# Attention's token stores on GpSimd's own queue, four units later, into sixteen arrays

## The chip, the cores and the metric

One core of one Trainium2 chip runs the whole program. The metric is the device time of one execution in microseconds (us), the median of several runs.

## The reference, cut to what matters

Attention with a decay bias runs first: 4 batches, 8 heads, 576 positions, head size 64. Its result, as 2304 tokens of width 512, goes through a first expert layer (2048 wide, squared ReLU) and a second one (three input matrices of width 768, of which the maximum is taken).

```python
cum = np.cumsum(np.maximum(s, 0.0), axis=-1)
bias = -(cum[:, :, :, None] - cum[:, :, None, :])
scores = np.where(causal, -1e9, scale * q @ k.T + np.minimum(bias, 0.0))
attn = exp(scores - max) / (sum + 1e-9)
x = (attn @ v).transpose(0, 2, 1, 3).reshape(2304, 512)
h = np.maximum(x @ moe_w_in, 0.0);            x = h * h @ moe_w_out
h = max(x @ w1, x @ w2, x @ w3);              out = h @ w_out
```

## The kernel before, in words

**Attention.** The 32 heads are taken as 16 pairs. A pair has nine units (`NU = 9`), each a block of 64 query rows of both heads (the last unit is the 64 rows of the tail), so there are 144 units. A unit passes through the stages scores (`u_s`), maximum (`u_max`), exponential (`u_exp`), transposition (`u_t`) and copy (`u_et`). Units are gathered in two windows for each pair: window 0 ends at unit 3 and window 1 at unit 8. A window passes through the stages `rc` (reciprocals of the sums), `pv` (the product with the values, L768, and a small transposition, L771), `out0`/`out1` (`w_out_`: VectorE copies the product to a buffer `ax`, L779, and the reciprocals to `rec`, L781), `keep` (SyncE writes the reciprocals to DRAM, L698 and L700), `rows` (SyncE reads them back spread over 128 partitions into a buffer `px`, L707), `px` (GpSimd multiplies `ax` by `px`, L786) and `xst` (the result is stored to the DRAM array `x_at`, L791).

**The order is written out by hand.** A list gives each stage its distance in units: at step n of the loop over units, the stage is issued for the window that ended at unit n + distance.

```python
ORDER = [("max", 1), ("rc", -4), ("out0", -6), ("out1", -7), ("exp", -1), ("et", -3), ("t", -2), ("s", 2), ("pv", -5), ("rows", -15),
         ("pump", 0), ("keep", -8), ("px", -21), ("xst", -23)]
```

Every engine takes its instructions strictly in the order of the program. SyncE (SP) does no arithmetic: in attention its queue holds nearly all transfers, one behind the other. For each pair these are the loads of `xk` (L600) and `xq` (L604), the four decay rows `ck` and `cq` (L611), the values `xv` in two parts (L618, L619), three `keep` writes, four `rows` reads and two `xst` stores. The loads of pair p are issued two pairs ahead, at the steps `LOADS = (1, 1, 2, 15)` counted from unit 0 of pair p - 2; `xv` is the one at 15, so it is issued 3 units before pair p begins, and `pv` of its window 0 comes at unit 3 with a distance of 5, thus 11 units behind that issue.

**Weights.** Beside attention, a planner (`Slots`, called by `pump` on six of nine units from unit 9 on) brings in weights of the first layer: two loads of 256 KB for each weight tile into `st` (L392), some word arithmetic on VectorE (L397 to L408), additions on GpSimd (L415, L433) and a cast on ScalarE (L429). In attention these loads go on SP's queue; from the expert phase on they go on GpSimd's, and the additions go to VectorE for jobs begun then.

**From attention to the experts.** The tokens 0 to 511 are read from `x_at` into `fx` (L817) and split (ScalarE L796, VectorE L799) while attention still runs; the first 24 matmuls of the first layer (L804) are laid between attention's last units. The first layer then visits the token chunks (512, 512, 512, 384, 384) in the order 0 to 4 and back 3 to 0. Each next chunk is read by `xload` (L890), 512 or 384 columns for each of the four feature blocks kk; the reads for the second visit are issued by ScalarE, all others by SP. Matmuls: L804 is the first product, ScalarE and VectorE (L963 to L966) make the squared activations `hh`, L987 is the second product.

`ax` has six buffers and `px` two; the pools of attention and of the experts lie in the same memory, one after the other. `x_at` is one DRAM array of [4, 128, 2304].

Of the kernel before, what the change touches and what calls it, by code (L numbers as in the profile page):

```python
# [8 lines left out]
F32 = mybir.dt.float32  # L9
# [41 lines left out]
PACE = 1.5  # L51
PACE_ATT = 5
ORDER = [("max", 1), ("rc", -4), ("out0", -6), ("out1", -7), ("exp", -1), ("et", -3), ("t", -2), ("s", 2), ("pv", -5), ("rows", -15),
         ("pump", 0), ("keep", -8), ("px", -21), ("xst", -23)]

# [189 lines left out]
def kernel(  # L247
# [15 lines left out]
    nc = tc.nc  # L263
    P = 128
    D = v_tail.shape[2]
    S = qT.shape[2]
    H = 8
    BH = s.shape[0]
    B = BH // H
    NT, DM = out.shape  # L270
    KD = DM // P
# [14 lines left out]

    perm = ctx.enter_context(tc.tile_pool(name="perm", bufs=1))
    dram = ctx.enter_context(tc.tile_pool(name="dram", bufs=1, space=bass.MemoryType.DRAM))
    x_at = dram.tile([KD, P, NT], F32, name="x_at")
    x_mid = dram.tile([KD, P, NT], F32, name="x_mid")  # L290
    part = dram.tile([KD, P, NT], F32, name="part")
    r_dram = [[dram.tile([2, (W0, W1)[w]], F32, name=f"r{w}{i}") for i in range(2)] for w in range(2)]
# [61 lines left out]
    def unit(n, i):  # L354
        _, q, j = items[n]
        return 7 * (3 * q + j) + i
# [141 lines left out]
    queue = [nc.sync]  # L498
# [14 lines left out]
    keep = {i: dram.tile([P, 1024], F32, name="keep_" + "_".join(map(str, i))) for i in second + late}  # L513
# [7 lines left out]
    phA = ExitStack()  # L521
# [1 line left out]
    at1 = phA.enter_context(tc.tile_pool(name="at1", bufs=1))  # L523
    small = phA.enter_context(tc.tile_pool(name="small", bufs=6))
    et_p = phA.enter_context(tc.tile_pool(name="et", bufs=2))
    px_p = phA.enter_context(tc.tile_pool(name="px", bufs=2))
    ax_p = phA.enter_context(tc.tile_pool(name="ax", bufs=6))
    fx_p = phA.enter_context(tc.tile_pool(name="fx", bufs=4))
    ring_s, ring_t = Ring(pairs[2:4]), Ring(pairs[0:2])

# [242 lines left out]
    ax_t = {}  # L773
# [14 lines left out]
    def w_xst(p, w):  # L788
        lo, hi = ((0, W0), (W0, S))[w]
        b, h = divmod(2 * p, H)  # L790
        nc.sync.dma_start(out=x_at[h // 2, :, b * S + lo:b * S + hi], in_=ax_t.pop((p, w))[:, 0:hi - lo])  # L791

    three = ((0, 0), (0, 1), (1, 0))

    def high(x, hi):
        nc.scalar.copy(out=hi, in_=x)  # L796

    def low_of(x, hi, lo):
        nc.vector.tensor_tensor(out=lo, in0=x, in1=f32(hi), op=ALU.subtract)  # L799
# [11 lines left out]
    fx = {}  # L811

    def first_split(kk, step):
        t0, n = chunks1[0]
        if step == 0:
            fx[kk] = fx_p.tile([P, 512], F32, tag="fx", name="fx")[:, 0:n]
            nc.sync.dma_start(out=fx[kk], in_=x_at[kk, :, t0:t0 + n])  # L817
        elif step == 1:
            first_x[kk] = tuple(slots_a[-1 - kk][:, i, :] for i in range(2))
            high(fx[kk], first_x[kk][0][:, 0:n])  # L820
        else:
            low_of(fx[kk], first_x[kk][0][:, 0:n], first_x[kk][1][:, 0:n])
# [5 lines left out]
    def attention():  # L828
# [3 lines left out]
        N = len(units)  # L832
        fns = dict(s=u_s, t=u_t, max=u_max, et=u_et, exp=u_exp)
        wfn = dict(rc=w_rc, pv=w_pv, out0=w_out_, out1=w_out_, keep=w_keep, rows=w_rows, px=w_px, xst=w_xst)
        span = max(abs(d) for _, d in ORDER)
        pre = first_products()
        coming = {}
        for n in range(-span, N + span + 1):
            if 0 <= n < N:
                p = n // NU  # L840
                for back in range(3):
                    if p + 2 - back < NP and p >= back:
                        to = p + 2 - back
                        if n == (to - 2) * NU + LOADS[0]:
                            coming[to] = loads(to)
                        for at, f in zip(LOADS, coming.get(to, ())):
                            if n == (to - 2) * NU + at:
                                f()
            for op, d in ORDER:
                if op == "pump":  # L850
                    if PUMP_FROM <= n < N + PUMP_END and n % NU in PUMP_U and (slots.free or slots.open):
                        slots.pump(1)
                elif op in wfn:
                    if n + d in wins and op not in ("out1", "out0")[wins[n + d][1]]:
                        wfn[op](*wins[n + d])
                elif 0 <= n + d < N:
                    fns[op](n + d)
            if n == N - PRE_AT:
                phQ.close()
                banks.extend(psum(ctx, "first", 2, [P, 512]))  # L860
            for kk in range(KD):
                for step, off in enumerate((-24, 0, 1)):
                    if n == N - PRE_X[kk] + off:
                        first_split(kk, step)
            if n >= N - PRE_AT:
                for _ in range(PRE_N):
                    next(pre, None)
# [3 lines left out]
    def experts():  # L871
# [15 lines left out]

        def xload(at, t0, n, kk):
            x = xr[at, kk] = xr_p.tile([P, 2 * T2], F32, tag="xr", name="xr")[:, 0:n]
            (nc.scalar if at == 1 else nc.sync).dma_start(out=x, in_=x_at[kk, :, t0:t0 + n])  # L890

        def xsplit(at, n, kk):
            x = xr.pop((at, kk))
# [29 lines left out]
        with ExitStack() as ph1:  # L923
# [11 lines left out]
            for kind, v, m, f in main1:  # L935
                ci, fs = visits[v]
                t0, n = chunks1[ci]
                end = m == len(fs) - 1
                nxt = chunks1[visits[v + 1][0]] if v + 1 < nv else None
                if kind == "h":  # L940
                    w = slots.get(("in", f))
# [8 lines left out]
                    if nxt:  # L950
                        for kk in range(KD):
                            if to_end == 7 - kk:
                                xload(v + 1, *nxt, kk)
                    elif to_end == 7:
                        for i in range(4):
                            raw_load(0, i)
# [12 lines left out]
                    if to_end in (5, 3):  # L969
                        kk = (5 - to_end) // 2  # L970
# [9 lines left out]
                else:  # L980
                    w = slots.get(("out", f))
# [30 lines left out]
        with ExitStack() as ph2:  # L1012
# [5 lines left out]
            at = {}  # L1018
# [91 lines left out]
            for item in main2:  # L1110
                if item[0] == "p":
                    _, m, i = item
# [3 lines left out]
                    b = where[i]  # L1116
                    if (m, b) not in at:
                        at[m, b] = rings[b].take()
                    w = slots.get(("p", unit(m, i) // 2))
                    at_w = unit(m, i) % 2 * 256  # L1120
                    x = ops[g, i]
# [16 lines left out]
                else:  # L1138
                    _, g, t, f, begin, end = item
# [69 lines left out]
```

## Time and profile before

| what | value |
|---|---|
| median of 3 runs | 859.21 us (856.16 to 860.18) |
| profiled execution, own time | 855.43 us |
| its span (first to last instruction) | 853.5 us, so 1.93 us lie around the span |
| granted TensorE clock, mean | 0.996 of full speed |
| attention with its last windows | about 0 to 191 us of the span |
| first layer's stream of matmuls | about 171 to 574 us |
| second layer | about 574 to 853 us |

The profile is one execution. Times in its rows are counted from the span's start. PE is TensorE, PEld its weight loads, DVE VectorE, ACT ScalarE, POOL GpSimd, SP SyncE; a trailing q means the engine's queue of instructions. L and a number is a line of the kernel.

### The profile page before, as it was taken

How to read it: one execution, taken by the hardware profiler on the slowest of the kernel's cores; microseconds unless marked ns; L12 is line 12 of the kernel's file. 1: busy time of each engine (PE TensorE's matmuls, PEld its weight loads, DVE VectorE, ACT ScalarE, POOL GpSimd, SP SyncE). 2: the span in 40 equal slices, each digit the busy share in tenths (PEclk: the TensorE clock that was granted, in tenths of full speed). 3: DMA queues.
4: the chain of work that ended last, by engine and by line, in shares of the span. 5: the costliest groups of instructions: out<-in, count | busy, mean ns of one | idle time of the engine just before them, and what ended most of it. 6: DMA issues, size and time to landing. Idle time of an engine off the chain costs nothing.

```text
span 853.5 us, 14429 instructions
## 1 busy us (share of the span) xinstructions
PE 829.5 (97%) x5284; PEld 702.8 (82%) x5284; DVE 525.6 (62%) x1103; ACT 408.4 (48%) x833; POOL 157.2 (18%) x241
## 2 busy tenths in 40 slices
PE   5999998898999999999999999999999999999998
PEld 3555554577888899999998888889998899989996
DVE  6778786837885566676687786753564235623442
ACT  5888887854544444445554454442233222421222
POOL 3042323325122333213222313100000000000000
PEclk9999999999999999999999999999999999999999
DMA  5555556544344553697658677729930573026602
GB/s 161 175 173 174 165 176 201 164 129 155 127 168 143 200 205 129 242 374 277 226 181 302 229 274 244 251 84 390 406 139 25 198 264 131 13 74 201 242 1 74
DMA packets 72246, 159.76 MB, mean 187 GB/s; under 512 B 11376, under 2 KB 31408, under 8 KB 72176
## 3 DMA queue, kind: packets, MB, share of 16 engines
q1 hardware_dynamic: 56340, 106.40, 36.2%
q0 software_dynamic: 15248, 51.39, 17.3%
q10 hardware_dynamic: 588, 1.06, 0.5%
q8 instruction: 41, 0.67, 0.3%
q14 instruction: 29, 0.24, 0.1%
HBM read 113.53 MB, written 45.27 MB: 186 GB/s over the span
## 4 chain that ended last, share of the span: by engine, by line
PE 88%; DMA 4%; DVE 3%; ACT 2%; SPq 1%; issue 1%; POOL 1%; ACTq 0%; POOLq 0%; DVEq 0%
PE banks L987 22%; PE banks L1124 13%; PE banks L804 11%; PE first L804 10%; PE banks L1096 9%; PE first L1124 8%; PE pairs L768 5%; PE pairs L723 3%; PE pair L644 2%; PE pairs L644 2%; DMA px<-r 1%; DMA st<-in_w_out_dram 1%; DMA xq<-in_qT_dram 1%; SPq L707 1%; PE pair L651 1%; PE pairs L651 1%
## 5 line engine op out<-in xcount | busy, mean ns | idle before, releaser
L987 PE MATMUL banks<-hh,sl 128*128 128x512 f32 (+1 forms) x960 | 211.6, 369 | 2.5 <-DVE hh L966 2.5
L987 PEld LDWEIGHTS banks<-hh,sl 128*128 128x128 f32 x960 | 176.1, 189 | 25.8 <-DVE hh L966 2.9
L1124 PE MATMUL banks<-xs,sl 128*128 128x384 f32 x702 | 131.2, 335 | 0.0
L1124 PEld LDWEIGHTS banks<-xs,sl 128*128 128x128 f32 x702 | 122.8, 188 | 0.9 <-DMA sl<-keep_p 0.2
L966 DVE TENSOR_TENSOR hh<-r,hh 128x512 fp32r<-128x512 f32 (+1 forms) x80 | 52.4, 656 | 99.6 <-ACT hh L965 99.4
L804 PE MATMUL first<-xs,sl 128*128 128x512 f32 (+1 forms) x432 | 93.6, 365 | 0.0
L804 PE MATMUL banks<-xs,sl 128*128 128x512 f32 (+1 forms) x432 | 93.6, 365 | 0.0
L681 ACT ACTIVATE e<-e,nm 128x128 f32<-128x128 f32 (+2 forms) x144 | 83.6, 585 | 12.3 <-DVE nm L667 12.1
L804 PEld LDWEIGHTS first<-xs,sl 128*128 128x128 f32 x432 | 78.6, 188 | 9.4
L804 PEld LDWEIGHTS banks<-xs,sl 128*128 128x128 f32 x432 | 78.6, 188 | 9.4
L1124 PE MATMUL first<-xs,sl 128*128 128x384 f32 x432 | 84.6, 335 | 0.0
L1096 PE MATMUL banks<-sl,hh 128*128 128x512 f32 (+1 forms) x342 | 78.4, 382 | 1.9 <-DVE hh L799 1.5
L1124 PEld LDWEIGHTS first<-xs,sl 128*128 128x128 f32 x432 | 75.8, 188 | 0.7 <-issue 0.3
L1096 PEld LDWEIGHTS banks<-sl,hh 128*128 128x128 f32 x342 | 61.4, 188 | 15.9 <-DVE hh L799 3.4
L963 ACT ACTIVATE r<-banks 128x512 f32<-128x512 f32 (+1 forms) x40 | 22.2, 556 | 93.9 <-PE banks L804 86.1
L963 ACT ACTIVATE r<-first 128x512 f32<-128x512 f32 (+1 forms) x40 | 22.2, 556 | 89.9 <-PE first L804 88.9
L768 PEld LDWEIGHTS pairs<-et,xv 128*64 128x64 f32 (+1 forms) x448 | 28.2, 136 | 34.8 <-ACT e L681 8.9
L768 PE MATMUL pairs<-et,xv 128*64 128x320 f32 (+4 forms) x448 | 53.2, 370 | 3.6 <-DVE nm L667 3.6
L1025 ACT COPY s<-first 128x384 f32<-128x384 f32 x36 | 17.2, 479 | 79.3 <-PE first L1124 79.2
L786 POOL TENSOR_TENSOR ax<-ax,px 128x256 f32<-128x256 f32 (+1 forms) x32 | 26.9, 840 | 120.6 <-DMA px<-r 93.8
L1025 ACT COPY s<-banks 128x384 f32<-128x384 f32 x45 | 21.6, 479 | 57.0 <-PE banks L1124 56.5
L964 ACT ACTIVATE r<-r 128x512 f32<-128x512 f32 (+1 forms) x80 | 47.2, 590 | 2.6
(108 smaller groups left out, 1154.6 us busy)
## 6 DMA issues: line engine op xcount, KB each, us to landing
sl<-keep_p SPq DMA_DIRECT2D x68, 512.0 KB
st<-in_w_dram POOLq DMA_DIRECT2D x36, 256.0 KB, 5.7
st<-in_w_out_dram POOLq DMA_DIRECT2D x35, 256.0 KB, 3.9
sl<-keep_out SPq DMA_DIRECT2D x14, 512.0 KB
keep_p<-hi POOLq DMA_DIRECT2D x9, 768.0 KB, 5.2
keep_p<-sums POOLq DMA_DIRECT2D x9, 768.0 KB, 6.1
st<-in_w_in_dram POOLq DMA_DIRECT2D x22, 256.0 KB, 4.2
xk<-in_kT_dram SPq DMA_DIRECT2D x16, 288.0 KB
```

Source lines behind the costliest of these rows:

```text
L644: nc.tensor.matmul(b[:, j, 0:w], lhsT=d["xq"][rows(j), w - P:w], rhs=d["xk"][rows(j), 0:w], start=True, stop=False)
L681: nc.scalar.activation(out=e_u[u][:, 0:w], in_=e_u[u][:, 0:w], func=ACTF.Exp, scale=-1.0, bias=st.pop(n), accum_out=sums[p, win][:, col:co ...
L768: nc.tensor.matmul(pv[rows(j), f:(W0, W1)[w]], lhsT=xv[0:kr, j, k, :], rhs=rhs, start=(k == 0), stop=(k == last))
L786: nc.gpsimd.tensor_tensor(out=x[:, 0:n], in0=x[:, 0:n], in1=rs_t.pop((p, w))[:, 0:n], op=ALU.mult)
L804: nc.tensor.matmul(hps[:, 0:n], lhsT=w[:, wp, kk * P:(kk + 1) * P], rhs=x[kk][xp][:, 0:n], start=(kk == 0 and c == 0), stop=(kk == KD - 1 ...
L963: nc.scalar.activation(out=r[:, 0:n], in_=hps[:, 0:n], func=ACTF.Relu)
L964: nc.scalar.activation(out=r[:, 0:n], in_=r[:, 0:n], func=ACTF.Square)
L966: nc.vector.tensor_tensor(out=hh[:, 1, 0:n], in0=r[:, 0:n], in1=f32(hh[:, 0, 0:n]), op=ALU.subtract)
L987: nc.tensor.matmul(xacc[d][:, 0:n], lhsT=w[:, wp, d * P:(d + 1) * P], rhs=hh[:, xp, 0:n], start=(m == 0 and c == 0), stop=(end and c == 2))
L1025: nc.scalar.copy(out=x, in_=bank[:, 0:T2])
L1096: nc.tensor.matmul(b, lhsT=hh[g, t][:, hp_, q, h, :], rhs=w[:, wp, lo:hi], start=(begin and n == h == c == 0), stop=(end and n == len(f) - ...
L1124: nc.tensor.matmul(at[m, b][:, 0:T2], lhsT=w[:, wp, at_w + kk * P:at_w + (kk + 1) * P], rhs=x[:, kk, xp, :], start=(i in (0, 1, 3) and kk ...
```

## The change

`px` and `xst` are both issued 25 units behind their window (they were at 21 and 23). The store goes on GpSimd's own queue instead of SP's, right behind the multiplication. `ax` gets eight buffers in place of six, `px` three in place of two. `x_at` becomes sixteen arrays [128, 576], by feature block (kk) and batch; so a read of tokens is cut at each multiple of 576 by a new function `tokens`, and chunks 1, 2 and 3 take two transfers for each block where they took one. `xload` uses SP's queue for all visits.

```diff
-         ("pump", 0), ("keep", -8), ("px", -21), ("xst", -23)]
+         ("pump", 0), ("keep", -8), ("px", -25), ("xst", -25)]
...
-    x_at = dram.tile([KD, P, NT], F32, name="x_at")
+    x_at = [[dram.tile([P, S], F32, name=f"x_at{k}{b}") for b in range(B)] for k in range(KD)]
...
-    px_p = phA.enter_context(tc.tile_pool(name="px", bufs=2))
-    ax_p = phA.enter_context(tc.tile_pool(name="ax", bufs=6))
+    px_p = phA.enter_context(tc.tile_pool(name="px", bufs=3))
+    ax_p = phA.enter_context(tc.tile_pool(name="ax", bufs=8))
...
-        nc.sync.dma_start(out=x_at[h // 2, :, b * S + lo:b * S + hi], in_=ax_t.pop((p, w))[:, 0:hi - lo])
+        nc.gpsimd.dma_start(out=x_at[h // 2][b][:, lo:hi], in_=ax_t.pop((p, w))[:, 0:hi - lo])
+
+    def tokens(queue, x, kk, t0, n):
+        at = t0
+        while at < t0 + n:
+            b, lo = divmod(at, S)
+            m = min(S - lo, t0 + n - at)
+            queue.dma_start(out=x[:, at - t0:at - t0 + m], in_=x_at[kk][b][:, lo:lo + m])
+            at += m
...
-            nc.sync.dma_start(out=fx[kk], in_=x_at[kk, :, t0:t0 + n])
+            tokens(nc.sync, fx[kk], kk, t0, n)
...
-            (nc.scalar if at == 1 else nc.sync).dma_start(out=x, in_=x_at[kk, :, t0:t0 + n])
+            tokens(nc.sync, x, kk, t0, n)
```

## Rows read from the trace of the kernel before

**Rows 1.** Part 1 of the page: busy us, share of span, instructions

```profile
PE 829.5 (97%) x5284; PEld 702.8 (82%) x5284; DVE 525.6 (62%) x1103; ACT 408.4 (48%) x833; POOL 157.2 (18%) x241
```

**Rows 2.** Windows in the expert phase: length, busy us by engine, PEclk, DMA

```profile
205.00:315.00 110.00, 110.00 (x490) 91.77 (x490) 79.28 (x138) 54.92 (x96) 28.45 (x54) 1.00 0.47 161
```

**Rows 3.** Windows from pair to pair (PE, PEld, DVE, ACT, POOL busy, PEclk, DMA)

```profile
119.22:128.81 9.59, 9.44 (x119) 5.60 (x119) 7.81 (x30) 8.62 (x26) 3.31 (x4) 1.00 0.52 148
128.81:143.44 14.63, 11.05 (x120) 6.82 (x119) 8.99 (x26) 10.03 (x27) 4.32 (x5) 0.88 0.64 201
143.44:155.44 12.00, 10.14 (x122) 5.93 (x122) 8.53 (x35) 9.68 (x26) 2.83 (x3) 1.00 0.67 192
155.44:165.56 10.12, 9.77 (x121) 5.74 (x122) 8.68 (x32) 8.19 (x23) 4.13 (x5) 1.00 0.51 156
...
sum 155.80, PE 149.18 PEld 89.45 DVE 115.71 ACT 130.71 POOL 46.12; mean PE 9.95 PEld 5.96 DVE 7.71 ACT 8.71 POOL 3.08
```

**Rows 4.** Timeline of PE, 120 to 160 us (start, us, ...)

```profile
133.62 0.22 PE L646 MATMUL pair<-ck,cq 64*128 64x128 bf16 x2
137.42 1.39 PE L768 MATMUL pairs<-et,xv 128*64 128x256 f32 x8 [3.58 <-DVE nm L667]
...
154.10 1.13 PE L644 MATMUL pair<-xk,xq 64*128 64x512 f32 x4 [1.48 <-DVE nm L667]
```

**Rows 5.** Timeline of ACT, 126 to 142 us

```profile
134.31 0.78 ACT L745 COPY et<-pairs 128x768 f32<-128x768 f32 x1
```

**Rows 6.** Timeline of SP's queue, attention

```profile
28.61 0.53 SPq L600 DMA_DIRECT2D xk<-in_kT_dram  x1
...
130.45 0.34 SPq L791 DMA_DIRECT2D x_at<-ax  x1
131.10 1.12 SPq L707 DMA_DIRECT2D px<-r  x2
132.32 0.53 SPq L618 DMA_DIRECT2D xv<-in_v_main_dram  x1
...
148.38 0.58 SPq L392 DMA_DIRECT2D st<-in_w_out_dram  x1
149.06 0.38 SPq L600 DMA_DIRECT2D xk<-in_kT_dram  x1
```

**Rows 7.** Timeline of DVE, 126 to 166 us

```profile
133.39 0.49 DVE L779 COPY ax<-pairs 128x320 f32<-128x320 f32 x1 [1.82 <-DMA x_at<-ax]
...
152.79 0.57 DVE L397 TENSOR_SCALAR wa<-st 128x512 uint32<-128x512 uint32 x1 [1.83 <-DMA st<-in_w_out_dram]
```

**Rows 8.** The line L791: duration in ns min/median/max, first and last start

```profile
L791 SPq DMA_DIRECT2D x_at<-ax x32: 325/341/525, 37.1 to 191.2; - x32
```

**Rows 9.** Waits of SP's queue: total us, times, longest

```profile
SPq L791 <- POOL ax L786: 5.9, 7, 2.9
```

**Rows 10.** The line L392 from 190 us on: GpSimd's own DMA issues

```profile
L392 POOL DMA_DIRECT2D st<-in_w_out_dram x35: 536/541/739, 192.4 to 542.4; - x35
```

**Rows 11.** The tile ax: GpSimd's multiplications

```profile
L786 POOL TENSOR_TENSOR ax<-ax,px x32: 726/859/1522, 30.7 to 190.3; 128x256 f32<-128x256 f32 x16, 128x320 f32<-128x320 f32 x16
```

**Rows 12.** Window in the expert phase where VectorE is full

```profile
215.00:220.00 5.00, 5.00 (x23) 4.14 (x23) 4.90 (x10) 2.38 (x4) 1.06 (x2) 1.00 0.31 105
```

**Rows 13.** Timeline of POOL, end of attention

```profile
190.32 0.88 POOL L786 TENSOR_TENSOR ax<-ax,px 128x320 f32<-128x320 f32 x1 [2.45 <-DMA px<-r]
191.15 1.29 POOL L433 TENSOR_TENSOR sl<-wa,sl 128x512 fp32r<-128x512 f32 x1
192.38 0.74 POOL L392 DMA_DIRECT2D st<-in_w_out_dram  x1
```

**Rows 14.** Timeline of DVE, 170 to 215 us

```profile
197.03 0.43 DVE L397 TENSOR_SCALAR wa<-st 128x512 uint32<-128x512 uint32 x1 [6.94 <-DMA st<-in_w_out_dram]
```

**Rows 15.** Timeline of PE, 165 to 215 us

```profile
202.88 4.18 PE L987 MATMUL banks<-hh,sl 128*128 128x512 f32 x11 [2.52 <-DVE hh L966]
```

**Rows 16.** Timeline of ACT, 170 to 215 us

```profile
185.31 0.60 ACT L963 ACTIVATE r<-banks 128x512 f32<-128x512 f32 x1 [4.27 <-DMA x_at<-ax]
```

## The prediction

> **What bounds the kernel now.** I read the page first. TensorE is busy for 829.5 of 853.5 us [rows 1], so only 24 us of the span can be won without changing its work. The windows of the expert phase show where they are not: over 110 us there PE is busy for all 110 [rows 2]. Whatever this change moves in the expert phase is therefore hidden as long as no wait grows to reach PE. The idle time must lie at the start (nothing here touches it), in attention, or between the two phases.
>
> Next I cut attention into windows from one pair's long `pv` product to the next [rows 3]. A pair takes about 9.6 us, PE full nearly throughout; the first row is the last such pair (9.59). The next three take 14.63, 12.00 and 10.12 us for the same work. Against 9.6 each they lose 5.03 + 2.40 + 0.52 = 7.95 us. In the worst one the granted clock falls to 0.88, between its two levels of 2.4 and 1.2 GHz, after PE had stood still: part of the 5.03 is slower work behind the wait.
>
> Then I asked what PE waited for there. The timeline of PE has two gaps: 3.58 us before an L768 at 137.42 and 1.48 us before an L644 at 154.10 [rows 4], both put down to VectorE's maximum. For the first that name can't be the cause: L768 reads `et` and `xv`, and no maximum. ScalarE's copy to `et` ended at 134.31 + 0.78 = 135.09 [rows 5]. What is left is `xv`, and SP's queue issued its load only at 132.32 [rows 6], 5.1 us before the product began. By the code the issue lies 11 units ahead of that product, at 9.6 / 9 = 1.07 us a unit 11.7 us; the product was due at 133.84, behind the last matmuls before the gap [rows 4], so the load was due at 122.1 and SP was 10.2 us late.
>
> Why is it late? Its `xk` loads, one for each pair, stand at 28.61 and, eleven pairs on, at 149.06 [rows 6]: (149.06 - 28.61) / 11 = 10.95 us a pair, where TensorE needs 9.6. SP falls behind by 1.35 us with each pair, and where the queue is read closely its issues stand nearly end to end [rows 6]. It eats up the distance by which loads were issued early, and from pair 12 on TensorE pays.
>
> The second gap has the same root by another way: VectorE stood for 1.83 us before L397 for a weight load [rows 7], issued on SP at 148.38 [rows 6], and the maximum that PE needed is behind L397. A third sign: VectorE stood for 1.82 us before L779, for a store of `x_at` that had to free one of the six `ax` buffers [rows 7].
>
> **The change part by part.**
>
> *Stores leave SP's queue.* 32 of them, two for each pair, of median 0.34 us [rows 8], and with them SP's waits for the multiplication, 5.9 us in all, or 0.37 for each of 16 pairs [rows 9]. SP's pace becomes 10.95 - 0.68 = 10.27 us by the issues alone and 9.90 with the waits. The lateness at pair 12, 10.2 us, shrinks in the ratio of the excess over 9.6: to 10.2 x 0.67 / 1.35 = 5.1 us, or 2.3. The load of `xv` then has 11.7 - 5.1 = 6.6 us or more, and needed 5.1. The weight load came 1.83 us too late for L397 and would come at least 5.1 earlier. Both gaps go, and with them the 0.52: -7.95 us.
>
> *Two more `ax` buffers and one more `px`.* A window holds `ax` from 6 or 7 to 25 units behind it, and the eighth next window comes 36 units later, so L779 finds a free buffer: the 1.82 us on VectorE go (they are inside the 7.95). `rows` of the third next window comes 13 or 14 units later, at 28 units from this one against its `px` at 25. That leaves SP 3 units, as before (24 against 21).
>
> *`px` four units later.* GpSimd's wait for `rows` moves into time in which SP is late anyway; nothing queues behind it in those units but additions for the weights. Costed at nothing; without that cover ScalarE's cast L429 and all behind it would wait.
>
> *The stores on GpSimd.* Such an issue takes 0.541 us there in the median, 0.739 at the most [rows 10]. GpSimd works 46.12 us over 15 pairs, 3.08 a pair [rows 3]; two stores make it 4.2 of 9.6. So it has room. One place has none: the last multiplication at 190.32 is followed by an addition and by the first weight load of the expert phase at 192.38 [rows 13]. VectorE stands 6.94 us for that load [rows 14], and behind it TensorE stands 2.52 us for `hh` [rows 15]. The last store comes between them, and every us there reaches PE: one issue of 0.54 and about 0.1 for the multiplication's end. The bounds are nothing (if the last `rows` arrives sooner) and 1.52, the longest thing that GpSimd did with that tile [rows 11]; I take 0.65, as the issue has rows of its own.
>
> Does GpSimd issue at 0.54 us while VectorE is busy? In the window at 215 VectorE works 4.90 of 5 us and GpSimd's 1.06 us there are two issues [rows 12], with the same word arithmetic as in attention. The Trainium skill (SBUF — State Buffer, SBUF: two separate sides) says that a GpSimd-issued DMA can be kept from writing its descriptors by a VectorE instruction in a two-port mode, and gives about 3100 ns in place of 620; its summary says to issue such a DMA from SP or ScalarE, which speaks against this change. The rows show no such stretch (739 ns at the most); by the page's figure the sum would lose another 2.5 us at the last store, an estimate.
>
> *ScalarE.* In the two slow pairs it worked 10.03 and 9.68 us [rows 3], as the split of the first tokens falls there: once PE no longer waits, ScalarE can hold these pairs to its own time. I charge 0.43 + 0.08 = 0.5 us; the bounds are nothing (rows of one engine overlap a little) and, if VectorE's order spoils it as well, 1.5.
>
> *Sixteen arrays and cut reads.* Three chunks, visited twice, four blocks each: 24 more issues on SP in the expert phase, hidden under PE's full windows [rows 2]. The reads for the second visit leave ScalarE, where the wait in front of one of them held L963 for 4.27 us [rows 16]; PE did not stand still then, so I give nothing for it. On SP they come behind the last `rows`, some us later than on ScalarE, but VectorE, whose split they feed, waits until 197.03 anyway [rows 14]. If that cover is gone, their delay adds to the 2.52 us.
>
> Sum: -7.95 + 0.65 + 0.5 = -6.8 us on the profiled execution's own 855.43, so 848.6. The median of the runs shown, 859.21, is 3.8 above that execution, and I carry the difference over: 859.2 - 6.8 = 852.4 us.
>
> **The rivals.**
>
> *The gap between the phases goes too.* If the last reciprocals come back sooner on a queue without stores, the weight load at 192.38 moves ahead and the 2.52 us shrink. For it: a store is issued between the last two `rows` on SP. Against it: the chain from the last product through two transfers to the multiplication is mostly latency. At the best -7.95 - 2.52 = -10.5: 848.7 us.
>
> *SP stays late.* If its pace is set by how fast transfers land, and not by the issues, the places of the stores fill with waits, `xv` comes as late as before, and only VectorE's 1.82 us [rows 7] are won: 857.4 us. For it: between the end of L791's issue at 130.79 and L707 at 131.10 SP waits 0.3 us though the buffer is old [rows 6]. Against it: from 130.45 to 132.85 the four issues take 1.99 of 2.40 us [rows 6], so issues, not waits, fill most of the queue. It decides if SP's lateness at pair 12 stays over 6.6 us.
>
> *GpSimd becomes the bound: slower.* GpSimd has 9.6 - 3.08 = 6.5 us a pair to spare, so it decides once a store holds its queue for over 3.26 us. At 4 us each a pair would take 11.08: 15 x 1.48 = 22 us more, less nothing won, 859.2 + 22 = 881 us. The additions for the weights would come late, ScalarE's L429 behind them, and its exponentials behind that. Against it: no issue over 0.739 us [rows 10] and no multiplication over 1.52 [rows 11]. By the skill's 3100 ns (the page named above), an estimate, it falls just short of that point.
>
> *Nothing seen.* ScalarE or VectorE take up what SP gives back: 855 to 860 us.
>
> **How the numbers follow.** Forecast 0.64 (its own range 849.5 to 855: the 0.65 and the 0.5 at their bounds, and 2 us for the median's own spread), the gap between phases too 0.10, SP stays late 0.14, nothing seen 0.05, GpSimd the bound 0.07. A measurement of this kernel can tell about 0.5%, 4.3 us, from no change. The first two cases are faster by more than that: 0.74. SP late and nothing seen are within it: 0.19. Slower: 0.07. The range reaches from below the second case, 846.5, to past the third, 858, and leaves out the slower case and the edges, some 2 in 10. I predict 852.4 us.
>
> **What would show it.** Right: windows from pair to pair near 9.6 us after 128 us too; `xk` loads on SP at 10.3 us or less; no gap at L768 with `xv` issued late; stores on GpSimd near 0.54 us; the gap before L987 of 2.5 to 3.5 us some 7 us earlier in the span. Wrong: SP's pace still near 10.9; stores on GpSimd over 1.5 us; a new wait of ScalarE for L415 or of VectorE for L796's result in the first visit; or a gap at the change of phases that has grown by what attention gave back.

## The result and the profile after

The changed kernel takes 847.44 us (median of 4 runs, 846.56 to 848.57) against 857.79 us for the kernel before (4 runs, 856.16 to 860.18): a ratio of 0.9878 with a 95% interval of 0.9847 to 0.9909, so 0.9 to 1.5% faster. The profiled execution takes 847.02 us, its span 845.2 us; before they were 855.43 and 853.5. The span is 8.3 us shorter.

TensorE's own work is nearly the same (829.5 us before [rows 1]); GpSimd has 18.2 us and 32 instructions more, the stores. Part 1 of the page of the changed kernel:

```profile
PE 826.4 (98%) x5284; PEld 700.5 (83%) x5284; DVE 524.3 (62%) x1103; ACT 407.5 (48%) x833; POOL 175.4 (21%) x273
```

**Attention.** Windows of the changed kernel from one pair's long `pv` product to the next, as in [rows 3]; the sum is that over all 15:

```profile
118.80:128.54 9.74, 9.74 (x120) 5.76 (x118) 8.49 (x30) 8.77 (x27) 5.23 (x6) 1.00 0.66 215
128.54:138.65 10.11, 9.77 (x120) 5.72 (x118) 7.47 (x30) 9.00 (x25) 4.99 (x6) 1.00 0.82 243
138.65:148.89 10.24, 9.87 (x121) 5.80 (x119) 7.99 (x31) 9.27 (x27) 5.42 (x7) 1.00 0.68 197
148.89:159.00 10.11, 9.76 (x120) 5.72 (x118) 9.13 (x32) 8.62 (x24) 3.37 (x4) 1.00 0.43 129
...
sum 149.76, PE 148.00 PEld 88.57 DVE 114.57 ACT 129.93 POOL 63.91; mean PE 9.87 PEld 5.90 DVE 7.64 ACT 8.66 POOL 4.26
```

The three slow pairs took 14.63 + 12.00 + 10.12 = 36.75 us before and take 10.11 + 10.24 + 10.11 = 30.46 us now. The 15 windows together give back 155.80 - 149.76 = 6.04 us, and the granted clock stays at 1.00.

SP's queue in the changed kernel, the rows that answer to [rows 6]:

```profile
28.25 0.52 SPq L600 DMA_DIRECT2D xk<-in_kT_dram  x1
...
123.42 0.53 SPq L618 DMA_DIRECT2D xv<-in_v_main_dram  x1
...
139.35 0.33 SPq L600 DMA_DIRECT2D xk<-in_kT_dram  x1
```

Eleven pairs take (139.35 - 28.25) / 11 = 10.10 us each instead of 10.95. And PE's timeline in the same stretch:

```profile
133.51 0.87 PE L768 MATMUL pairs<-et,xv 128*64 128x256 f32 x8
134.88 0.72 PE L723 MATMUL pairs<-identF,e 64*128 64x64 f32 x16 [0.35 <-ACT et L745]
144.99 0.71 PE L723 MATMUL pairs<-identF,e 64*128 64x64 f32 x16 [0.35 <-ACT et L745]
155.22 0.71 PE L723 MATMUL pairs<-identF,e 64*128 64x64 f32 x16 [0.35 <-ACT et L745]
```

The product that stood 3.58 us [rows 4] has no wait in brackets any more: its `xv` was issued 133.51 - 123.42 = 10.1 us ahead, where it had been 5.1. What is left are three waits of 0.35 us for ScalarE's copy.

**GpSimd's stores.** The line L791 (ns min/median/max), and two lines of the table of waits (us in total, times, longest):

```profile
L791 POOL DMA_DIRECT2D x_at<-ax x32: 581/581/736, 31.6 to 182.8; - x32
```

```profile
POOL ax L786 <- DMA px<-r: 37.9, 6, 22.6
POOL x_at L791 <- POOL ax L786: 9.5, 32, 0.3
```

A store is issued in 0.58 us, 0.74 at the most, and waits 0.30 us each time for the end of the multiplication ahead of it: 0.88 us of GpSimd's time, 1.76 a pair.

**Between the phases.** PE from the last `pv` product on, first in the kernel before, then in the changed one:

```profile
178.29 2.42 PE L768 MATMUL pairs<-et,xv 128*64 128x320 f32 x20
...
206.89 2.88 PE L804 MATMUL banks<-sl,sl 128*128 128x512 f32 x12
```

```profile
171.81 2.42 PE L768 MATMUL pairs<-et,xv 128*64 128x320 f32 x20
...
195.68 2.79 PE L995 MATMUL banks<-hh,sl 128*128 128x512 f32 x11 [1.82 <-DVE hh L974]
198.31 2.88 PE L812 MATMUL banks<-sl,sl 128*128 128x512 f32 x12
```

The way from that product to the block behind the gap took 206.89 - 178.29 = 28.60 us and now takes 198.31 - 171.81 = 26.50, 2.10 less. The wait is 1.82 instead of 2.52 us, and the 11 matmuls behind it take 2.79 instead of 4.18 us [rows 15]. Windows over just those 11, before and after, show why the same matmuls differ (the third figure from the right is the granted clock):

```profile
202.88:206.89 4.01, 4.01 (x11) 3.23 (x12) 3.94 (x5) 1.74 (x4) 3.51 (x6) 0.62 0.52 179
```

```profile
195.68:198.31 2.63, 2.63 (x11) 2.18 (x12) 2.56 (x5) 0.86 (x2) 1.53 (x4) 1.00 0.73 238
```

Behind the longer wait the granted clock was 0.62 in the mean, between its two levels and nearer to the lower one of 1.2 GHz; behind the shorter one it was at 2.4 throughout. So of the 2.10 us, 0.70 are the wait and 1.39 the clock. Attention's 6.04 and these 2.10 make 8.14 of the 8.3 us.

### The profile page after: what moved, and what is told of

Its sections match the earlier page's. It is cut to its first block, busy times and chain, and to the rows that moved or that the text cites. A ratio compares the mean times of both kernels' runs of the same rounds, so it can differ in the third digit from the quotient of the medians.

```text
span 845.2 us, 14494 instructions
## 1 busy us (share of the span) xinstructions
PE 826.4 (98%) x5284; PEld 700.5 (83%) x5284; DVE 524.3 (62%) x1103; ACT 407.5 (48%) x833; POOL 175.4 (21%) x273
## 2 busy tenths in 40 slices
DMA packets 72631, 159.77 MB, mean 189 GB/s; under 512 B 12784, under 2 KB 32816, under 8 KB 72560
## 4 chain that ended last, share of the span: by engine, by line
PE 91%; DVE 3%; ACT 2%; DMA 2%; POOL 1%; issue 0%; SPq 0%; DVEq 0%; ACTq 0%; POOLq 0%
PE banks L995 22%; PE banks L1132 13%; PE first L812 11%; PE banks L812 11%; PE banks L1104 9%; PE first L1132 8%; PE pairs L768 5%; PE pairs L723 3%; PE pairs L644 2%; PE pair L644 2%; PE pair L651 1%; ACT e L681 1%; DMA st<-in_w_in_dram 1%; PE pairs L651 1%; DVE hh L807 1%; PE pairs L646 1%
## 5 line engine op out<-in xcount | busy, mean ns | idle before, releaser
L995 PE MATMUL banks<-hh,sl 128*128 128x512 f32 (+1 forms) x960 | 210.1, 367 | 1.8 <-DVE hh L974 1.8
L995 PEld LDWEIGHTS banks<-hh,sl 128*128 128x128 f32 x960 | 175.1, 188 | 24.8 <-DVE hh L974 2.2
L973 ACT CAST hh<-r 128x512 fp32r<-128x512 f32 (+1 forms) x80 | 46.3, 579 | 2.5
```

The lines of the kernel that those rows point to most:

```text
L973: nc.scalar.copy(out=hh[:, 0, 0:n], in_=r[:, 0:n])
L995: nc.tensor.matmul(xacc[d][:, 0:n], lhsT=w[:, wp, d * P:(d + 1) * P], rhs=hh[:, xp, 0:n], start=(m == 0 and c == 0), stop=(end and c == 2))
```

## The experiments

Each ratio is to the kernel before, measured beside it. The experiments came in three groups, the first four (the stores on SP, the queue alone, `rows`, the first kernel with the reads on ScalarE), the next four (the store that waits for nothing, the last two stores, the split, the early one with more buffers) and the last two; differences under about 0.5% between kernels of different groups are not read.

### The stores back on SP, late, with all the buffers

```diff
-         ("pump", 0), ("keep", -8), ("px", -25), ("xst", -25)]
+         ("pump", 0), ("keep", -8), ("px", -25), ("xst", -27)]
...
-        nc.gpsimd.dma_start(out=x_at[h // 2][b][:, lo:hi], in_=ax_t.pop((p, w))[:, 0:hi - lo])
+        nc.sync.dma_start(out=x_at[h // 2][b][:, lo:hi], in_=ax_t.pop((p, w))[:, 0:hi - lo])
```

> The changed kernel with the stores back on SP's queue (two units behind the multiplication, as before), and all else of the change kept: eight and three buffers, the later places, sixteen arrays. Theory (SP's pace decides): SP's xk loads fall back to 10.8 us a pair or more, xv comes late again, TensorE has gaps of some 3 us in pairs 12 to 14; 853 to 857 us, ratio to the kernel before 0.995 to 1.0. Rival (the buffers and the later places made the gain, as they free VectorE from its 1.82 us wait for a store): like the changed kernel, 0.988.

856.55 us, ratio 1.0001 (0.9984 to 1.0019). The whole gain is gone: buffers, the later place and the sixteen arrays together win nothing while SP issues the stores. Its `xk` loads stand 10.87 us apart (28.65 to 148.18). The profiled execution, 852.45 us, is one of its fastest, and still has one pair as slow as the worst before; the longest wait in it is that of L644 for VectorE's maximum (windows and waits of this kernel):

```profile
139.63:154.01 14.38, 10.21 (x120) 5.88 (x118) 8.98 (x36) 10.00 (x27) 2.86 (x3) 1.00 0.64 191
```

```profile
PE pair L644 <- DVE nm L667: 2.6, 1, 2.6
```

### GpSimd's queue alone: four units earlier, six and two buffers

```diff
-         ("pump", 0), ("keep", -8), ("px", -25), ("xst", -25)]
+         ("pump", 0), ("keep", -8), ("px", -21), ("xst", -21)]
...
-    px_p = phA.enter_context(tc.tile_pool(name="px", bufs=3))
-    ax_p = phA.enter_context(tc.tile_pool(name="ax", bufs=8))
+    px_p = phA.enter_context(tc.tile_pool(name="px", bufs=2))
+    ax_p = phA.enter_context(tc.tile_pool(name="ax", bufs=6))
```

> Stores on GpSimd's queue with sixteen arrays, but multiplication and store at 21 units and six and two buffers: the queue alone. Theory: SP's pace about 10 us a pair, pairs near 9.6 to 10.2 after 128 us, 847 to 850 us, ratio 0.988 to 0.991. Rival (the four units are needed, as GpSimd stands in front of the reciprocals' rows and the weights' additions come late): 853 us or more, ratio over 0.994.

851.5 us, ratio 0.995 (0.9933 to 0.9968): some 0.5% where the whole change gives 1.2%, so the queue alone gives under half of it. The time lies between the two that were expected, 1.5 us over the theory's upper end and 1.5 under the rival's; the ratio is on the rival's side (over 0.994). SP's pace is (142.54 - 28.77) / 11 = 10.34 us, between the two. Two things are worse than in the changed kernel. GpSimd stands for `rows` 20 times instead of 6 (waits), and the wait between the phases is 3.02 us with a slow clock behind it (the granted clock of 199.00 to 203.20 is 0.59):

```profile
POOL ax L786 <- DMA px<-r: 69.2, 20, 23.5
```

```profile
199.00 4.37 PE L995 MATMUL banks<-hh,sl 128*128 128x512 f32 x11 [3.02 <-DVE hh L974]
```

### Early, but with eight and three buffers

The changed kernel with `("px", -21), ("xst", -21)` and nothing else changed.

> The changed kernel with multiplication and store back at 21 units, buffers eight and three kept. Theory (in the run with the queue alone, GpSimd stood 69 us for the rows, against 38 in the changed kernel, and its additions came late): like that run, 850 to 852 us, ratio 0.995. Rival (the third px buffer, which frees SP's rows from waiting for GpSimd, made the difference): like the changed kernel, 848 us.

850.69 us, ratio 0.993 (0.9911 to 0.9949). The buffers don't replace the four units. The loss is in attention: its 15 pairs take 154.22 us, 4.46 more than in the changed kernel, and the spans differ by 849.7 - 845.2 = 4.5. SP's pace is 10.72 us (29.09 to 147.03), GpSimd stands 21 times for `rows` (84.0 us in all), and in attention VectorE once stands 3.8 us for a weight load (from the waits in 28 to 150 us):

```profile
DVE wa L397 <- DMA st<-in_w_in_dram: 3.8, 1, 3.8
```

### A store on SP that waits for nothing

To tell SP's time for issuing from its wait for the multiplication, each window gets one more store on SP, of a constant tile into an array that nobody reads. The real stores stay on GpSimd.

```diff
+        extra = dram.tile([P, W1], F32, name=f"extra{p}{w}")
+        nc.sync.dma_start(out=extra[:, 0:hi - lo], in_=bound_l[:, 0:hi - lo])
```

> The changed kernel with two issues for each pair put back on SP's queue that wait for nobody: a store of a constant tile (the same 128 and 160 KB) to arrays that nobody reads. The tokens are still stored by GpSimd. Theory (it is the issue time on SP's queue that counts): SP's pace is 10.3 us a pair or more, xv comes late again, attention loses 2 to 5 us, 850 to 853 us, ratio 0.991 to 0.995. Rival (it is the store's wait for the multiplication that held SP, not its 0.34 us): like the changed kernel, 847.5 us, 0.989 or less.

861.2 us, ratio 1.0049 (1.0032 to 1.0066): all of the gain lost and 0.5% more, worse than either theory expected. The issues are dearer than the stores of before: 0.58 us in the median, against 0.34 [rows 8].

```profile
L792 SPq DMA_DIRECT2D extra<-bound_l x32: 422/582/1122, 39.4 to 191.6; - x32
```

Two of them are 2 x 0.58 = 1.16 us a pair, and SP's pace goes from 10.10 to (153.70 - 28.53) / 11 = 11.38, 1.28 more. Nothing waits for these stores and they wait for no arithmetic, so the slots on SP's queue count. The extra stores also move 4.7 MB more (164.50 MB in the profiled execution, against 159.77), and what that costs was not told apart. It can't be what the stores cost on SP in the first experiment, which moves the same 159.77 MB as the changed kernel. PE now stands openly for `xv` (waits of PE, 60 to 200 us):

```profile
PE pairs L768 <- DMA xv<-in_v_main_dram: 3.0, 4, 1.7
```

### `rows` instead of the stores leave SP

The kernel before, with its stores on SP as they were and the 64 reads `rows` on GpSimd:

```diff
-            nc.sync.dma_start(out=rs[rows(j), 0:cols], in_=d[j:j + 1, :].to_broadcast([D, cols]))
+            nc.gpsimd.dma_start(out=rs[rows(j), 0:cols], in_=d[j:j + 1, :].to_broadcast([D, cols]))
```

> The kernel before, with the stores left on SP, but the four rows reads for each pair (0.56 us each on SP) issued by GpSimd: SP is relieved by another part. Theory (any relief of SP's queue does it): SP's pace under 9.7, no gap in pairs 12 to 14, 850 to 852 us, ratio 0.990 to 0.993; the gap between the phases stays near 2.5 us. Rival (the stores themselves or the buffers matter): 856 us or more, ratio over 0.997.

852.0 us, ratio 0.9949 (0.9931 to 0.9968). The time is as expected and the reason is not. SP does get faster, to 10.31 us a pair where under 9.7 was expected, but attention as a whole does not: its 15 pairs take 155.55 us, as before [rows 3]. That sum hides two things. An early pair, and the three that were slow before:

```profile
61.00:73.92 12.92, 11.15 (x121) 6.68 (x119) 10.12 (x32) 9.17 (x25) 5.21 (x8) 0.87 0.59 188
...
132.96:143.35 10.39, 9.84 (x121) 5.81 (x119) 8.08 (x30) 9.42 (x27) 5.99 (x8) 1.00 0.77 226
143.35:154.62 11.27, 9.87 (x121) 5.81 (x119) 8.89 (x31) 9.27 (x26) 5.73 (x8) 1.00 0.60 180
154.62:164.73 10.11, 9.76 (x120) 5.72 (x119) 9.13 (x32) 8.55 (x23) 4.99 (x7) 1.00 0.40 122
```

The three slow pairs take 31.77 us instead of 36.75: relief of SP by quite another part gives back 4.98 us just where SP was late. But the early pair takes 12.92 us where a pair takes 9.6, and the others lose some more. The timelines of PE, VectorE and GpSimd in the early pair show a small operation of VectorE that takes 2.28 us:

```profile
68.61 0.22 PE L771 MATMUL pairs<-identF,sm 64*4 64x64 f32 x2 [1.77 <-DVE sm L692]
```

```profile
66.07 2.28 DVE L691 TENSOR_SCALAR sm<-sm 128x4 f32<-128x4 f32 x1
```

```profile
66.45 1.05 POOL L415 TENSOR_TENSOR wa<-st 128x512 f32<-128x512 f32 x1
67.45 0.86 POOL L786 TENSOR_TENSOR ax<-ax,px 128x320 f32<-128x320 f32 x1
```

What is left of the gain came between the phases: the wait before L987 is 0.36 us, and the 11 matmuls behind it take 2.79 us.

### Where the reads of tokens are issued, and the last two stores

Two kernels. In the first the reads for the first expert visit go on ScalarE's queue. The second does that too, and issues the last pair's two stores on SP.

```diff
-            tokens(nc.sync, x, kk, t0, n)
+            tokens(nc.scalar if at == 1 else nc.sync, x, kk, t0, n)
```

> The changed kernel with the reads for the second visit back on ScalarE's queue. Theory (the 2.1 us won between the phases come from the reciprocals' way on a queue without stores): the same as the changed kernel within 1 us, ratio 0.988. Rival (they come from ScalarE, which no longer stands for 4.27 us): the gap before the second product's fourth block is back at 2.5 us, 849.5 us, ratio 0.990.

848.33 us, ratio 0.9919 (0.9897 to 0.9942): nothing that can be told from the changed kernel. Attention takes 149.79 us, the wait between the phases is 2.10 us, and the 11 matmuls behind it take 2.79. So what was won between the phases does not come from these reads leaving ScalarE.

```diff
-        nc.gpsimd.dma_start(out=x_at[h // 2][b][:, lo:hi], in_=ax_t.pop((p, w))[:, 0:hi - lo])
+        (nc.sync if p == NP - 1 else nc.gpsimd).dma_start(out=x_at[h // 2][b][:, lo:hi], in_=ax_t.pop((p, w))[:, 0:hi - lo])
```

> The changed kernel, but the last pair's two stores go on SP's queue and the reads for the second visit on ScalarE's (alone they changed little). Theory (GpSimd's last two stores, 0.9 us each with the wait for the multiplication's end, stand in front of the first weight load): that load comes 1.8 us earlier, the gap of 1.8 to 2.1 us before the second product shrinks to under 1 us, 846 to 847 us, ratio about 0.987. Rival (the gap is set by VectorE's own row of work, not by the load): no change, 848.3 us.

845.58 us, ratio 0.9875 (0.986 to 0.9891). A second time, beside the kernel with one array below:

> The changed kernel with the reads of tokens of the first expert visit on ScalarE's queue and the last pair's two stores on SP, once more, beside the one-array kernel on the same chip. Theory (the last two stores cost 0.9 us on GpSimd's way into the expert phase, and SP is free there): 845 to 847 us, 1 to 2.5 us under the changed kernel. Rival (its lead over the changed kernel was that of one chip): 847 to 849 us, within 0.15% of the changed kernel.

845.56 us, ratio 0.9879 (0.9862 to 0.9896); its runs, 845.10 to 846.05, lie below all five of the one-array kernel beside it (847.42 to 852.25). PE's wait before L995 is no longer in the trace in either run. GpSimd's end of attention, first in the changed kernel, then with the last two stores on SP:

```profile
179.97 0.73 POOL L786 TENSOR_TENSOR ax<-ax,px 128x256 f32<-128x256 f32 x1 [7.81 <-DMA px<-r]
180.99 0.58 POOL L791 DMA_DIRECT2D x_at<-ax  x1 [0.30 <-POOL ax L786]
181.60 0.88 POOL L786 TENSOR_TENSOR ax<-ax,px 128x320 f32<-128x320 f32 x1
182.78 0.58 POOL L791 DMA_DIRECT2D x_at<-ax  x1 [0.30 <-POOL ax L786]
183.38 1.30 POOL L433 TENSOR_TENSOR sl<-wa,sl 128x512 fp32r<-128x512 f32 x1
184.61 0.56 POOL L392 DMA_DIRECT2D st<-in_w_out_dram  x1
```

```profile
181.60 0.87 POOL L786 TENSOR_TENSOR ax<-ax,px 128x320 f32<-128x320 f32 x1 [0.54 <-DMA px<-r]
182.44 1.29 POOL L433 TENSOR_TENSOR sl<-wa,sl 128x512 fp32r<-128x512 f32 x1
183.68 0.58 POOL L392 DMA_DIRECT2D st<-in_w_out_dram  x1
```

From the multiplication's end (182.48) to the addition (183.38) the store costs 0.90 us; without it the addition follows at once. This is the fastest kernel of the study.

### The split of the first tokens on GpSimd

The three waits of 0.35 us behind ScalarE stand in the pairs in which it splits the first tokens. GpSimd takes the cast:

```diff
-            high(fx[kk], first_x[kk][0][:, 0:n])
+            nc.gpsimd.tensor_copy(out=first_x[kk][0][:, 0:n], in_=fx[kk])
```

> The changed kernel with the high parts of the first tokens (four casts of 128x512) made by GpSimd in place of ScalarE. Theory (the 0.5 us that each pair after 128 us still loses are ScalarE's casts of 0.62 us): these pairs come back to 9.6 to 9.75 us, 1.5 us won, 845.5 to 846.5 us. Rival (GpSimd's work holds VectorE, and the casts come late for it): the pairs stay over 10 us, 847 us or more.

847.83 us, ratio 0.9904 (0.9887 to 0.9922): no gain. ScalarE's waits are gone, and longer ones for VectorE's reciprocals and copies stand in their place (waits of PE):

```profile
PE pairs L771 <- DVE sm L692: 1.1, 2, 0.7
PE pairs L723 <- DVE rec L781: 0.8, 2, 0.5
```

### One array of tokens

The changed kernel with `x_at` as one array [4, 128, 2304], its reads cut as in the change.

> The changed kernel with one array of tokens instead of sixteen; queue, place and buffers as changed. Theory (SP's issue slots and the place of the stores decide, how the tokens are cut in DRAM decides nothing): within 0.5% of the changed kernel, 845.5 to 850 us against its 847.4, stores on GpSimd still 0.58 us each, the pairs from the sixth on still 9.6 to 10.3 us apart. Rival (with one array each read of the expert phase is ordered behind all of the stores, the last one included, and the reads of the first blocks start late): the reads of tokens start after the last store lands, 2 us or more later in the change of phases, 849.5 us or more.

848.62 us, ratio 0.993 (0.9907 to 0.9952), which meets the interval of the changed kernel only at its edge; but the median is 1.2 us above it, 0.14%, and the profiled span 845.6 against 845.2. All pairs but the last are 9.6 to 10.3 us apart, as in the changed kernel, and the wait between the phases is 2.27 us. The sixteen arrays add little or nothing; these runs can't tell which.

## Why the prediction was right, and where it was not

**The bound was SP's queue: shown.** With the stores on SP all the gain is gone (1.0001), and stores on SP that depend on nothing cost more than the gain (1.0049). Taking `rows` off SP instead gives the three slow pairs 4.98 us back, and loses almost as much in other places. The forecast pace of 9.90 to 10.27 us a pair holds the 10.10 found, and the `xv` load came 10.1 us ahead of its product, enough by the 5.1 that it needs. The rival that SP stays late is out: by the same count as before, `xv` was due 11.7 us ahead of 133.51, at 121.8, and is 1.6 us late instead of 10.2, less than the 2.3 to 5.1 forecast.

The lower end of that pace, though, came from a misread row. The 5.9 us that SP waits for the multiplication [rows 9] are of the whole run; from 28 to 165 us the row is

```profile
SPq L791 <- POOL ax L786: 1.7, 5, 0.4
```

That is 0.15 us a pair and not 0.37, so the pace to expect was 10.95 - 0.68 - 0.15 = 10.12 us, and 10.10 was found.

**The term of 7.95 us was taken too large against its own correction.** The three pairs gave back 36.75 - 30.46 = 6.29. They stop at 10.11 to 10.24 us, 1.66 above 3 x 9.6, where I had charged 0.5 for ScalarE (its bound was 1.5). The three 0.35 us waits are 1.05 of the 1.66. The third pair did not move at all: 10.12 us before, 10.11 now. Its 0.52 was never SP's, and PE's timeline of the kernel before has the same wait for ScalarE's copy there:

```profile
161.71 0.72 PE L723 MATMUL pairs<-identF,e 64*128 64x64 f32 x16 [0.35 <-ACT et L745]
```

The split on GpSimd showed that these waits go and others come. Whether VectorE would have been right behind ScalarE anyway, or is held by the casts on GpSimd, was not told apart.

**"Costed at nothing" was wrong for the four units.** The step said that GpSimd's wait for `rows` moves into time in which SP is late anyway. At 21 units GpSimd stood 20 or 21 times for them, at 25 only 6 times; before it was 23. The place alone doesn't do that: at 25 units, but with stores back on SP or extra ones there, GpSimd stood 20 and 24 times. The two early kernels have profiled spans of 849.8 and 849.7 us and no run under 848.72; of the changed kernel and the three that differ from it only in the split, the reads or the array, the spans are 844.9 to 846.1 and the medians 847.44 to 848.62. Within their groups the queue alone, which lacks the buffers too, stands 851.5 - 848.33 = 3.2 us above the kernel with its reads on ScalarE, and the early kernel with all buffers 850.69 - 847.83 = 2.9 above the one with the split on GpSimd, though the intervals of each two overlap a little. So the four units are worth some 2 to 4 us. That GpSimd's waits pass on to the weights is argued from the one 3.8 us wait for a weight load. SP's own waits say where its pace goes: in front of `rows` (L707) it stands 6.0 us in the changed kernel from 28 to 165 us, but 11.5 with the queue alone and 12.8 with all buffers. The profile puts most of these waits down to loads of `xk` and `xq`, which `rows` does not read, so what holds it there stays open. The four units help only with the stores off SP: on SP they gave nothing.

**Between the phases the sign was wrong.** I had charged +0.65 us for the last store ahead of the first weight load, and the store costs 0.90; most of the difference is the wait for the multiplication's end, 0.30 us where I had taken 0.1 from no row. But the stretch became 2.10 us shorter, since the chain ahead of that store is shorter. SP's queue at the end of attention, before and after:

```profile
183.15 0.35 SPq L791 DMA_DIRECT2D x_at<-ax  x1
183.55 1.13 SPq L707 DMA_DIRECT2D px<-r  x2
184.78 0.53 SPq L791 DMA_DIRECT2D x_at<-ax  x1
185.49 1.11 SPq L707 DMA_DIRECT2D px<-r  x2
```

```profile
175.96 0.59 SPq L700 DMA_DIRECT2D r<-rec  x1
176.65 2.40 SPq L707 DMA_DIRECT2D px<-r  x4
```

The issue of the last `rows` ended 186.60 - 178.29 = 8.31 us behind the start of the last `pv` product, with two stores ahead, and ends 179.05 - 171.81 = 7.24 us behind it now. The last multiplication starts 9.79 us behind that product instead of 12.03 [rows 13], a lead of 2.24 us of which the store takes 0.90 back. This is the first rival's mechanism, given a chance of 0.10. I had argued against it that the chain is mostly latency; 1.07 us of it were two places in the queue. The other 1.17 us lie behind the issue of `rows`, where the multiplication now starts 2.55 us later instead of 3.72; why was not tried. The wait of PE shrank by only 0.70, but the clock stayed up behind it, worth 1.39 more, a price that no term of mine had. The length of a wait alone doesn't tell what the clock does: in attention a wait of 1.77 us (`rows` on GpSimd) was followed by a granted clock of 0.87 in that pair, while one of 2.6 us (the stores back on SP) stands in a pair at 1.00. So that the 0.70 us are what kept the clock up is argued, not shown. Without the last two stores on GpSimd the rest of the wait goes too.

**GpSimd as the bound:** no issue over 0.74 us in attention, no stretch like the rival's. The Trainium skill (SBUF — State Buffer, SBUF: two separate sides) lets an issue be held by VectorE; no row here shows that.

**The sum.** On the profiled executions I forecast -6.8 us and measured 847.02 - 855.43 = -8.4, 1.6 more: attention gave 6.0 where I had 7.45, and the phases between gave 2.1 where I had a loss of 0.65. On the medians the miss is larger, 852.4 against 847.44, outside the forecast's own range of 849.5 to 855. The other 3.4 us are the difference that I carried over: the median of before stood 3.8 us above its profiled execution, that of the changed kernel 0.4 above its own. The range of 846.5 to 858 held it only because it had been drawn to reach below the first rival's 848.7. The upper end of the forecast's own range is off as well: with the two terms at their bounds and 2 us of spread it would have been 856.3 and not 855.

## What to carry to other kernels

A queue that only issues can be the bound: take the distance between like instructions on it over many rounds, and compare that with the pace of the engine it feeds. When an issue leaves such a queue, count the slots that it frees on every chain through that queue, the last one of the phase above all. On the queue that takes it over, look for the one place where somebody waits behind it: there alone, leave it where it was.

## What the runs showed of the hardware that was not expected

**A tiny operation of VectorE can last as long as a GpSimd operation beside it.** L691 works on 128x4 or 128x5 numbers in 0.17 us (median of 32). In the changed kernel it takes 0.84 us when it starts inside a GpSimd operation, and ends just behind it, at 95.66 (timelines of VectorE and GpSimd):

```profile
94.82 0.84 DVE L691 TENSOR_SCALAR sm<-sm 128x4 f32<-128x4 f32 x1
```

```profile
94.37 1.27 POOL L433 TENSOR_TENSOR sl<-wa,sl 128x512 fp32r<-128x512 f32 x1 [1.79 <-ACT sl L429]
```

In the kernel with `rows` on GpSimd it took 2.28 us, to the end of two GpSimd operations that stand end to end, and PE stood 1.77 us behind it. Its row starts 0.38 us ahead of the first of the two, while GpSimd was issuing two `rows` (65.36 to 66.44). By the Trainium skill (SBUF — State Buffer, Who interferes with whom) a `tensor_scalar` of VectorE can run in a two-port mode, and then whichever of it and a GpSimd operation issues first gets the port pair that they share and the other fully blocks. The 0.84 us agree with that; the 2.28 us do only if GpSimd's issues count too. Neither that, nor that L691 runs in such a mode, is shown by a row here. I had weighed only the other one, VectorE against GpSimd's issues, of which no row shows anything.

**An issue's price differs with the queue, and between two kinds of store on one queue.** The same stores took 0.34 us on SP [rows 8] and 0.58 on GpSimd, and the stores of a constant tile on SP 0.58 as well. It is not the sixteen arrays: back on SP, the stores into them took 0.34 us in the median. Why the two kinds on SP differ was not tried.
